# A gated linear attention and its feed-forward layer on one core: units of three chunks in a hand-written order, against single chunks in an order planned by the program

## The chip, the core and the metric

The kernel runs on one core of a Trainium2 chip (trn2). The metric is the device time of one execution in microseconds (us); smaller is better. The program is one instruction stream for each engine: TensorE (PE in the profile, its weight loads PEld), VectorE (DVE), ScalarE (ACT), GpSimd (POOL) and SyncE (SP). Each engine works through its stream strictly in the order in which the kernel wrote it, so an instruction that waits holds up all that stands behind it on that engine. SP only issues transfers (DMAs); POOL issues some too, beside its own arithmetic.

## What is computed

Inputs are q, k, v, a_re and a_im, each of shape (4, 8, 768, 48): 4 batches, 8 heads, 768 steps, 48 channels; and a feed-forward layer with weights of 384x1536 and 1536x384. For each batch and head a 48x48 state is decayed by a complex gate, gets the product k v added, and is read with q. Cut to what matters:

```python
mag = np.sqrt(a_re * a_re + a_im * a_im)
scale = np.minimum(mag, 0.999) / (mag + 1e-06)
a_re_n, a_im_n = (a_re * scale, a_im * scale)
for t in range(S):
    new_re = ar * S_re - ai * S_im
    new_im = ar * S_im + ai * S_re
    S_re, S_im = (new_re + kv, new_im)
    y[:, :, t] = np.einsum('bhd,bhde->bhe', q[:, :, t], S_re)
...
xn = (x - mu) / np.sqrt(var + 1e-06) * g_ln
out = x + np.maximum(xn @ w_ch1, 0.0) @ w_ch2      # x: the 8 heads of y side by side, (4, 768, 384)
```

Both kernels turn the recurrence into a product over chunks of 128 steps. With L the running sum of ln(magnitude) and theta the running sum of the angles, q is multiplied by exp(L)cos(theta) and exp(L)sin(theta), k by exp(-L) and the same two, and a masked 128x128 product of the two takes the place of the loop inside a chunk. A state of 128x384 (decayed by the last row of exp(L), called the edge) goes from one chunk to the next. There are 24 chunks, 6 in each batch.

## The kernel before

A *unit* is three chunks; there are eight. The gate work of a unit is done on 128x1152 tiles (three chunks wide):

- `e_ln` (L175): ACT takes Ln of a_re and Exp of minus that, which is 1/a_re. `e_r` (L180): DVE forms r = a_im/a_re and r squared. `e_l1p` (L185): ACT takes Ln(1 + r squared). `e_lm` (L188): DVE adds 2 Ln(a_re) and caps the sum. So the magnitude comes from a_re and the ratio.
- `e_exp` (L198): per chunk, a matmul with a triangular matrix makes the running sum, ACT takes Exp with both signs; after the unit's last chunk a small DMA on SP (L207) fetches the edge row.
- `e_atan`, `e_carry`, `e_phase`, `e_trig` (L210 to L249): arctan, running sum of angles in turns (carried from chunk to chunk through `carry`), ACT moves it out of PSUM with 768 added (tile w), three DVE operations on the low 16 bits fold it to one turn (f, g), ACT takes two Sin.
- `e_qk`, `e_stack` (L251 to L262): DVE multiplies q and k with exp, sine and cosine: six products in bf16.
- `heads_t` (L264): 16 transposes on PE into two PSUM tiles; ACT copies one out (qt, L273), DVE the other (kt).

Then per chunk: `scores` (L278: 8 matmuls, DVE applies the mask), `values` (L289: y, the state's update, and at a unit's first chunk the decay from the edge, L308 to L312), `norm_t` (L329: x is transposed on PE, DVE copies it out as xt and takes mean and variance). Per unit and block of 128 hidden columns: `up` (L346: three matmuls of 384 columns, ACT applies Relu). Per chunk `down` (L358: 12 matmuls, DVE adds the residual, SP stores).

ACT needs one set of tables for Ln and Exp and another for arctan and sine; `table` (L164) loads them.

The order is written by hand: `put(s, i, f, ...)` (L401) hangs gate work on slot i of step s, and the loop over steps (L467) interleaves it with `values`, `up`, `norm_t`, `scores` and `down`. `up` runs a unit behind, `down` two units behind. For batch b the gates of both its units start five steps before (LEAD, L24). `fold` (L134), which works the layer-norm gain and mean into w1c, is put at step 3 (L423), but its first multiplications depend only on the weights' arrival and may be written earlier into DVE's stream.

Transfers: a_re and a_im go through SP, one DMA of 1,024 rows of 192 bytes for each chunk; q, k, v go through POOL, which converts them to bf16 on the way, also one for each chunk. Two buffers hold units of a_re and a_im, three those of q, k, v. `gln` and `w1c` (L128, L129) come behind the 18 loads of units 0 and 1 on POOL; `w2b` (L132) at step 0.

Of the kernel before, what the change touches and what calls it, by code (L numbers as in the profile page):

```python
# [11 lines left out]
F16 = mybir.dt.float16  # L12
# [3 lines left out]
PI = 3.14159265358979323846  # L16
LNCAP = -0.0020010006671670786
TWO_PI_SAFE = 6.2831845
PI_SAFE = 3.14159225

TURNS = 768.0
TURN = 1 << 14
INV2PI = 1.0 / (2.0 * PI)
LEAD = 5  # L24
MM, SM = 3, 3
NOSYNC = mybir.DependencyInfo(mybir.DependencyClass.NoSync, mybir.DependencyReason.DATA)
# [3 lines left out]
def kernel(  # L30
# [15 lines left out]
    NCH = S // C  # L46
    DM = H * D
# [4 lines left out]
    UC = 3  # L52
    NU = NCH // UC
    UT = UC * C

# [6 lines left out]
    xs = pool("xs", 10)  # L62
    moe = pool("moe", 2)


    units = [{"b": U // NU, "u": U % NU, "U": U} for U in range(B * NU)]
    source = {"ar": (a_re, FP32, nc.sync, 2), "ai": (a_im, FP32, nc.sync, 2),
              "q": (q, BF16, nc.gpsimd, 3), "k": (k, BF16, nc.gpsimd, 3),
              "v": (v, BF16, nc.gpsimd, 3)}

    def load(U, names, c=None):
        if U >= B * NU:
            return
        st = units[U]
        for n in names:
            ap, dt, eng, bufs = source[n]
            view = ap[st["b"]].rearrange("h (c p) d -> p h c d", p=C)
            if n not in st:
                st[n] = ins.tile([C, H, UC, D], dt, tag=n, name=n, bufs=bufs)
            for i in range(UC) if c is None else (c,):  # L80
                eng.dma_start(out=st[n][:, :, i], in_=view[:, :, st["u"] * UC + i])  # L81


    for c in range(UC):
        load(0, ("ar", "ai"), c)
    ident = consts.tile([C, C], BF16)
    make_identity(nc, ident)
    u_half = consts.tile([C, C], BF16)
    make_upper_triangular(nc, u_half, val=0.5, diag=True)
    u_turn = consts.tile([C, C], BF16)  # L90
    make_upper_triangular(nc, u_turn, val=INV2PI, diag=True)
    mask = consts.tile([C, C], BF16)
    make_upper_triangular(nc, mask, val=1.0, diag=True)

    def const(val, shape, dt=FP32, name=None):
        t = consts.tile(shape, dt, name=name)
        nc.vector.memset(t, val)
        return t

    one_b = const(1.0, [C, 1], name="one_b")  # L100
    turns = const(TURNS, [C, 1], name="turns")
    pi_b = const(PI_SAFE, [C, 1], name="pi_b")
    mhalf_pi = const(-PI / 2.0, [C, 1], name="mhalf_pi")
    all_turn = const(INV2PI, [C, C], BF16, name="all_turn")
    ones = const(1.0, [C, C], BF16, name="ones")
    mhalf = const(-0.5, [C, UC], name="mhalf")

    kstks, edgs = [], []
    qstk = consts.tile([C, UC, H, 2, DP], BF16)
    nc.vector.memset(qstk[:, :, :, :, D:DP], 0.0)  # L110
    for i in range(2):
        ks = consts.tile([C, UC, H, 2, DP], BF16, name=f"kstk{i}")
        nc.vector.memset(ks[:, :, :, :, D:DP], 0.0)
        kstks.append(ks)
    for i in range(4):
        ed = consts.tile([UC * H, DP], BF16, name=f"edge{i}")
        nc.vector.memset(ed, 0.0)
        edgs.append(ed)

    load(0, ("q", "k", "v"))  # L120
    load(1, ("ar", "ai"))
    load(1, ("q", "k", "v"))


    w1c = consts.tile([C, ND, DF], BF16)
    w2b = consts.tile([C, NJ, DM], BF16)
    gln = consts.tile([C, ND], FP32)
    nc.gpsimd.dma_start(out=gln, in_=moe_g_ln.rearrange("(i p) -> p i", p=C))  # L128
    nc.gpsimd.dma_start(out=w1c, in_=moe_w_ch1.rearrange("(i p) j -> p i j", p=C))  # L129

    def load_w2():
        nc.gpsimd.dma_start(out=w2b, in_=moe_w_ch2.rearrange("(j p) e -> p j e", p=C))  # L132

    def fold(n):  # L134
        blk = w1c[:, :, ts(n, 512)]
        for i in range(ND):
            nc.vector.tensor_scalar(out=blk[:, i], in0=blk[:, i], scalar1=gln[:, ds(i, 1)],
                                    scalar2=None, op0=ALU.mult)
        ps = psum.tile([C, 512], FP32, tag="mm", name="w_ps", bufs=MM)
        for i in range(ND):  # L140
            nc.tensor.matmul(ps, lhsT=ones, rhs=blk[:, i], start=(i == 0), stop=(i == ND - 1))
        mean = moe.tile([C, 512], BF16, tag="mean", name="mean")
        nc.scalar.activation(out=mean, in_=ps, func=AF.Copy, scale=-1.0 / DM)
        for i in range(ND):
            nc.vector.tensor_tensor(out=blk[:, i], in0=mean, in1=blk[:, i], op=ALU.add)


    ALL = slice(0, UC)
    chunks, state, carry = {}, [None], [None]
    chd = lambda t, cs: t[:, :, cs].rearrange("p h c d -> p c h d")  # L150
    row = lambda x, c: x[:, c].rearrange("p h d -> p (h d)")
    fm = lambda x: x.rearrange("p c h d -> p (c h) d")
    small_ps = lambda name, dt=FP32: psum.tile([C, DM], dt, tag="s", name=name, bufs=SM)

    def utile(st, name, dt=BF16, tag=None, bufs=None):
        if name not in st:
            st[name] = el.tile([C, UC, H, D], dt, tag=tag or name, name=name, bufs=bufs)
        return st[name]


    tables = {"exp": "natural_log_exp_and_others", "trig": "trig_and_small"}
    group = [None, []]

    def table(name):  # L164
        p = nc.scalar.preload_act_table_set(tables[name])  # L165
        for i in group[1]:
            tc.add_manual_dep(p.ins, i.name, NOSYNC, reason="table order")
        group[:] = [p, []]

    def act(**kw):  # L170
        i = nc.scalar.activation(**kw)  # L171
        tc.add_manual_dep(i.ins, group[0].ins.name, NOSYNC, reason="table order")
        group[1].append(i.ins)

    def e_ln(st, cs=ALL):  # L175
        ar = chd(st["ar"], cs)
        act(out=ar, in_=ar, func=AF.Ln)
        act(out=utile(st, "rec", FP32, "wide", 3)[:, cs], in_=ar, func=AF.Exp, scale=-1.0)

    def e_r(st, cs=ALL):  # L180
        r, r2 = utile(st, "r")[:, cs], utile(st, "r2", tag="tmp", bufs=4)[:, cs]
        nc.vector.tensor_tensor(out=r, in0=chd(st["ai"], cs), in1=st["rec"][:, cs], op=ALU.mult)  # L182
        nc.vector.tensor_tensor(out=r2, in0=r, in1=r, op=ALU.mult)

    def e_l1p(st, cs=ALL):  # L185
        act(out=chd(st["ai"], cs), in_=st["r2"][:, cs], func=AF.Ln, bias=one_b)

    def e_lm(st, cs=ALL):  # L188
        if "lm" not in st:
            st["lm"] = el.tile([C, H, UC, D], BF16, tag="lm", name="lm")  # L190
        hcd = lambda t: t[:, :, cs].rearrange("p h c d -> p h (c d)")
# [21 lines left out]
    def e_carry(st, cs=ALL):  # L213
        for c in range(cs.start, cs.stop):
            if st["u"] == 0 and c == 0:
                carry[0] = None
# [298 lines left out]
```

## Time and profile before

| what | us |
|---|---|
| two timed runs, median | 259.5 and 260.24, 259.87 |
| span of the profiled execution, first to last instruction | 259.0 |
| busy in that span: PE / DVE / ACT / POOL | 181.4 / 182.3 / 180.5 / 79.5 |
| first matmul of `up` (h_ps, L354) starts | 86.3 |
| last matmul ends | 255.5 |
| w1c lands | 45.7 |

The profiled execution has no timed figure beside its span; the span is 0.9 us under the median of the timed runs. A time in the profile counts from the span's start. "Releaser" is what ended an engine's wait. In the strip of 40 slices each slice is 6.5 us wide and a digit is the busy share in tenths.

### The profile page before, as it was taken

What the parts mean: (1) busy time and instruction counts of PE and PEld (TensorE: products, weight loads), DVE (VectorE), ACT (ScalarE), POOL (GpSimd) and SP (SyncE); (2) the same over time, 40 slices, a digit from 0 to 9 for tenths busy, and PEclk for the clock granted to TensorE, in tenths of its full rate; (3) what the DMA queues carried; (4) which work ended last, traced back from release to release, by engine and by line L of the source; (5) the groups of instructions that cost most, each with busy time, mean ns of one, the idle gap of its engine ahead of it and who ended that gap; (6) DMA issues with size and microseconds to landing.
All of it is one profiled execution on the core that took longest, in us unless ns stands there. A gap on an engine that the chain in (4) does not pass through costs nothing.

```text
span 259.0 us, 4791 instructions
## 1 busy us (share of the span) xinstructions
PE 181.4 (70%) x1844; PEld 123.9 (48%) x1845; DVE 182.3 (70%) x374; ACT 180.5 (70%) x292; POOL 79.5 (31%) x103
## 2 busy tenths in 40 slices
PE   0116600330227976879999599999969999999994
PEld 0004500210226544666666467666647776766662
DVE  4448960930699889999978999986798966663121
ACT  4568820293978989999879999767988645435430
POOL 9944444761453088520450801032000100101000
PEclk9999965555558979999999999999979999999999
DMA  8999999999997699890699950037000101000112
GB/s 119 146 135 135 136 154 184 145 182 156 138 109 153 123 146 90 41 48 30 98 179 203 145 54 32 33 42 67 31 3 0 63 9 55 33 33 34 59 61 91
DMA packets 130551, 23.93 MB, mean 92 GB/s; under 512 B 125536, under 2 KB 130144, under 8 KB 130528
## 3 DMA queue, kind: packets, MB, share of 16 engines
q0 software_dynamic: 76864, 9.44, 57.0%
q1 hardware_dynamic: 53664, 14.18, 30.4%
q8 instruction: 14, 0.23, 0.3%
q14 instruction: 9, 0.07, 0.1%
HBM read 28.31 MB, written 4.72 MB: 128 GB/s over the span
## 4 chain that ended last, share of the span: by engine, by line
PE 39%; ACT 23%; DMA 21%; DVE 11%; issue 3%; POOL 2%; SPq 0%; ACTq 0%; DVEq 0%; POOLq 0%
PE o_ps L364 16%; PE h_ps L354 11%; DMA w1c<-in_moe_w_ch_dram 6%; DMA q<-in_q_dram 6%; DMA ar<-in_a_re_dram 5%; ACT qt L273 4%; ACT ht L356 4%; PE qk_ps L272 4%; DMA k<-in_k_dram 3%; ACT ar L171 2%; DVE qstk L261 2%; ACT L165 2%; ACT rec L171 2%; ACT w L171 2%; PE a_ps L285 2%
## 5 line engine op out<-in xcount | busy, mean ns | idle before, releaser
L354 PE MATMUL h_ps<-xt,w1c 128*128 128x384 bf16 x288 | 57.5, 329 | 1.2 <-ACT qt L273 0.9
L356 ACT ACTIVATE ht<-h_ps 128x384 bf16<-128x384 f32 x96 | 44.6, 505 | 10.0 <-PE h_ps L354 9.9
L364 PE MATMUL o_ps<-w2b,ht 128*128 128x384 bf16 x288 | 50.2, 326 | 0.3 <-ACT ht L356 0.3
L287 DVE TENSOR_TENSOR at<-a_ps,mask 128x512 bf16<-128x512 f32 x48 | 31.6, 678 | 7.3 <-PE a_ps L285 7.3
L364 PEld LDWEIGHTS <-ht 128*128 128x128 bf16 x288 | 27.6, 98 | 17.2 <-issue 0.4
L81 POOL DMA_DIRECT2D v<-in_v_dram x24 | 21.3, 895 | 46.3 <-PE t_ps L318 27.9
L354 PEld LDWEIGHTS <-w1c 128*128 128x128 bf16 x288 | 26.6, 98 | 17.3 <-issue 3.8
L81 POOL DMA_DIRECT2D k<-in_k_dram x24 | 21.8, 921 | 29.3 <-DVE en L255 13.2
L201 PE MATMUL l_ps<-lm,u_half 128*128 128x384 bf16 x24 | 7.9, 365 | 32.5 <-DVE lm L195 30.3
L367 DVE SCALAR_TENSOR_TENSOR o<-o_ps,rs,x 128x384 f32<-128x384 f32 x24 | 14.7, 614 | 21.6 <-PE o_ps L364 19.3
L273 ACT COPY qt<-qk_ps 128x1024 bf16<-128x1024 bf16 x24 | 24.3, 1024 | 6.0 <-PE y_ps L299 3.3
L341 POOL TENSOR_SCALAR rs<-mv 128x3 f32<-128x3 f32 x8 | 3.3, 410 | 76.2 <-DVE dec L311 54.9
L272 PE MATMUL qk_ps<-ident,qstk 128*128 128x128 bf16 x192 | 17.1, 240 | 12.4 <-DVE qstk L261 11.6
L171 ACT ACTIVATE ep<-l_ps 128x384 bf16<-128x384 f32 x24 | 12.2, 508 | 16.4 <-PE l_ps L201 16.3
L81 POOL DMA_DIRECT2D q<-in_q_dram x24 | 21.9, 924 | 5.5 <-DMA k<-in_k_dram 4.5
L302 ACT CAST x<-y_ps 128x384 bf16<-128x384 f32 x24 | 11.7, 489 | 16.3 <-PE y_ps L299 14.2
L182 DVE TENSOR_TENSOR r<-ai,rec 128x1152 bf16<-128x1152 f32 (+1 forms) x10 | 11.1, 1109 | 14.8 <-ACT rec L171 8.1
L272 PEld LDWEIGHTS <-qstk 128*128 128x128 bf16 x192 | 14.0, 109 | 15.2 <-DVE qstk L261 13.2
L230 PE MATMUL th_ps<-r,u_turn 128*128 128x384 bf16 x24 | 8.9, 394 | 15.6 <-ACT r L171 8.4
L285 PE MATMUL a_ps<-qt,kt 128*128 128x128 bf16 x192 | 17.5, 223 | 2.3 <-DVE at L287 1.7
L334 PEld LDWEIGHTS <-x 128*128 128x128 bf16 x72 | 5.8, 101 | 27.6 <-issue 23.8
L273 DVE COPY kt<-qk_ps 128x1024 bf16<-128x1024 bf16 x24 | 16.2, 680 | 2.9 <-PE qk_ps L272 2.9
(79 smaller groups left out, 390.2 us busy)
## 6 DMA issues: line engine op xcount, KB each, us to landing
ar<-in_a_re_dram SPq DMA_DIRECT2D x24, 192.0 KB, 4.5
ai<-in_a_im_dram SPq DMA_DIRECT2D x24, 192.0 KB, 8.2
out_dram<-o SPq DMA_DIRECT2D x24, 192.0 KB, 1.9
q<-in_q_dram POOLq DMA_DIRECT2D x24, 96.0 KB, 4.9
k<-in_k_dram POOLq DMA_DIRECT2D x24, 96.0 KB, 9.5
v<-in_v_dram POOLq DMA_DIRECT2D x24, 96.0 KB, 5.9
w1c<-in_moe_w_ch_dram POOLq DMA_DIRECT2D x1, 1152.0 KB, 16.3
w2b<-in_moe_w_ch_dram POOLq DMA_DIRECT2D x1, 1152.0 KB, 15.1
```

The source lines that it names most:

```text
L81: eng.dma_start(out=st[n][:, :, i], in_=view[:, :, st["u"] * UC + i])
L171: i = nc.scalar.activation(**kw)
L182: nc.vector.tensor_tensor(out=r, in0=chd(st["ai"], cs), in1=st["rec"][:, cs], op=ALU.mult)
L272: nc.tensor.transpose(t_ps[:, h], x[:, c, h].rearrange("p a d -> p (a d)"), ident)
L273: copy(out=o, in_=t_ps)
L285: nc.tensor.matmul(a_ps[:, j], lhsT=ch["kt"][:, h], rhs=ch["qt"][:, h], start=True, stop=True)
L287: nc.vector.tensor_tensor(out=at[:, ts(i, H // 2)], in0=a_ps, in1=mask_b, op=ALU.mult)
L302: nc.scalar.copy(out=x, in_=y_ps)
L354: nc.tensor.matmul(h_ps, lhsT=w1c[:, i, ts(j, C)], rhs=st["xt"][:, i], start=(i == 0), stop=(i == ND - 1))
L356: nc.scalar.activation(out=st["ht"][:, j], in_=h_ps, func=AF.Relu)
L364: nc.tensor.matmul(o_ps, lhsT=st["ht"][:, j, ts(c, C)], rhs=w2b[:, j], start=(j == 0), stop=(j == NJ - 1))
L367: nc.vector.scalar_tensor_tensor(out=o, in0=o_ps, scalar=st["rs"][:, ds(c, 1)], in1=chunks[U * UC + c]["x"], op0=ALU.mult, op1=ALU.add)
```

## The change

The kernel is rewritten; the algorithm of the chunks stays. What differs:

1. **A planner.** Each piece of work is declared with engine, an assumed duration, what it needs and makes, and a due time; `Plan.order` runs a list schedule on these assumed times and the instructions are written in that order. The transfers of a queue are modelled as a ring of their own (`QY`, `QP`); issuing one is assumed to cost 0.1 us on SP and 0.9 us on POOL.
2. **Chunks, not units.** `up` works on one chunk: 36 matmuls of 128 columns each instead of 36 of 384 for three chunks; ACT applies Relu to 1,024 and 512 columns at once. Gates are worked in groups: chunks 0; 1 and 2; 3 to 5 of batch 0, then three at a time.
3. **Magnitude from the sum of squares.** m2 = a_re² + a_im², L = half of Ln(m2); 1/a_re = Exp(-0.5 Ln(a_re²)). In batch 0 ACT squares and DVE adds and multiplies; from batch 1 on GpSimd does all four operations (two squares, the sum, the angle's ratio), and the adding of carries.
4. **Phases from mid-batch.** From batch 1 on the running angle starts at the batch's middle and runs backwards over its first half (`u_back`, `all_back`), so that 192 turns added to it keep enough bits; DVE moves it out of PSUM with that addition, ACT takes Sin of the low 16 bits directly, and DVE adds a quarter turn for the second. Only group 2 (`far`) still shifts.
5. **Smaller moves.** The first step of `fold` goes from DVE to ACT. From chunk 10 on x is transposed by a DMA issued on SP, not on PE. The loads of w1c and w2b move ahead on POOL, and one DMA loads all six chunks of a tensor for batches 2 and 3.

The core of the diff:

```diff
+    def load(eng, b, names, c=None, after=()):
+            op(eng, 0.1 if eng is Y else 0.9 if c is not None else 4.0, list(before.get(eng, ())) + list(after),
+               [key] + [("in_" + n, b)], load_fn, eng, b, n, c)
+            plan.add(RING[eng], (2.04 if b < 2 else 1.5) * len(cs), None, [key],
+                     [("got_" + n, b, i) for i in cs], lag=2.0)
...
-    def e_ln(st, cs=ALL):
-        ar = chd(st["ar"], cs)
-        act(out=ar, in_=ar, func=AF.Ln)
-        act(out=utile(st, "rec", FP32, "wide", 3)[:, cs], in_=ar, func=AF.Exp, scale=-1.0)
...
+    def gate_exp(G, eng, early):
+        n, g = G["n"], G["i"]
+        sb = 0.2 + 0.32 * n
+        slow = 0.1 + 0.42 * n if eng is V else 0.2 + 0.8 * n
...
+        sq = (A, sb) if eng is V else (eng, slow)
+        op(*sq, got("ar"), [("ar2", g)], e_ar2, uses=[in_("ar")])
+        op(*sq, got("ai"), [("ai2", g)], e_ai2, uses=[in_("ai")])
+        op(eng, slow, [("ar2", g), ("ai2", g)], [("m2", g)], e_m2, uses=[in_("ar")])
+        act(sb, [("ar2", g)], [("ln", g), rw], e_ln, uses=[in_("ar")])
+        act(sb, [("ln", g)], [("rec", g)], e_rec, uses=[rw])
+        op(eng, slow, got("ai") + [("rec", g)], [("r", g)], e_r, uses=[in_("ai"), rw])
+        act(sb, [("m2", g)], [("lm0", g)], e_lm, **kw)
+        op(V, 0.1 + 0.13 * n, [("lm0", g)], [("lm", g)], e_cap, **kw)
...
+        op(Y, 0.1, [("ep", g), ("consts",)], [("edge", g)], e_edge, lag=2.5)
...
+            op(V, 0.1 + 0.42 * m, [("th_ps", g, j)], [("w", g), rw], e_turn, j, m, **kw)
...
+        act(sb, [src], [("sin", g)], e_sin, "sin", uses=[rw], **kw)
+        op(V, 0.1 + 0.21 * n, [("w", g), ("sin", g)], [("w2", g)], e_quarter, uses=[rw], **kw)
...
+        if j == 0:
+            op(T, 0.1, [("edge", G["i"])], [("e_ps", g)], decay, takes="nar")
+            op(V, 0.12, [("e_ps", g)], [("dec", G["i"])], decay_out)
...
+        if g < PE_X:
+            op(T, 0.18, [("x", g)], [("x_ps", g)], x_turn, takes="nar")
+            op(V, 0.36, [("x_ps", g)], [("xt", g)], xt_out)
+        else:
+            op(Y, 0.1, [("x", g)], [("xt", g)], xt_dma, lag=3.0)
...
+        for j0, j1 in ((0, 8), (8, 12)):
+            op(T, 0.163 * (j1 - j0), [("xt", g)] + w1, [("h_ps", g, j0)], up, j0, j1,
+               takes="wide" if j1 - j0 > 4 else "nar")
+            op(A, 0.2 + 0.107 * (j1 - j0), [("h_ps", g, j0)], [("ht", g)], relu, j0, j1)
...
+        op(T, 1.97, [("ht", g), ("W2",)], [("o_ps", g)], down, takes="nar")
+        op(V, 0.61, [("o_ps", g), ("rs", u), ("x", g)], [("o", g)], residual)
+        op(Y, 0.1, [("o", g)], [("out", g)], store, due=40.0 + STEP * g)
...
+    for c in range(GMAX):
+        load(Y, 0, ("ar", "ai"), c)
+    op(P, 1.5, [], [("consts",)], constants)
+    load(P, 0, ("q", "k", "v"), 0)
+    load_w(P, 0.1, ("gln",), gln, moe_g_ln.rearrange("(i p) -> p i", p=C))
+    load(P, 0, ("q", "k", "v"), 1)
+    load_w(P, 10.0, ("W1",), w1c, moe_w_ch1.rearrange("(i p) j -> p i j", p=C))
+    load(P, 0, ("q", "k", "v"), 2)
+    for c in range(GMAX, NCH):
+        load(Y, 0, ("ar", "ai"), c)
+    load(P, 0, ("q", "k", "v"), 3)
+    load_w(P, 12.0, ("W2",), w2b, moe_w_ch2.rearrange("(j p) e -> p j e", p=C))
+    for c in range(GMAX + 1, NCH):
+        load(P, 0, ("q", "k", "v"), c)
+    for c in range(NCH):
+        load(Y, 1, ("ar", "ai"), c, [("edge", 0)] if c < 3 else [("edge", 1)])
+        load(P, 1, ("q", "k", "v"), c)
+    for b in range(2, B):
+        load(Y, b, ("ar", "ai"))
+        load(P, b, ("q", "k", "v"))
...
+    phases = [([G], V) for G in groups[:3]] + [([G], P) for G in groups[3:5]] + [
+        (groups[2 * b + 1:2 * b + 3], P) for b in range(2, B)]
...
+    done = plan.order(SLOTS)
+    with tc.manual_schedule():
+        for o in done:
+            if o["fn"]:
+                o["fn"][0](*o["fn"][1])
```

Here V, A, P, T and Y are DVE, ACT, POOL, PE and SP; `STEP` is 6.9, `PE_X` 10. Groups are numbered 0 to 8; group 3 is the first of batch 1. Buffers of each of the five inputs hold a whole batch, two of them.

## The prediction

> **What bounds the kernel now.** First the strip of 40 slices on the profile's page. Read it for where PE, which does most of the arithmetic, is idle.
>
> ```profile
> PE   0116600330227976879999599999969999999994
> DVE  4448960930699889999978999986798966663121
> ACT  4568820293978989999879999767988645435430
> POOL 9944444761453088520450801032000100101000
> PEclk9999965555558979999999999999979999999999
> DMA  8999999999997699890699950037000101000112
> ```
>
> PE is nearly idle for thirteen slices (some 85 us) and nearly full afterwards; in that first part the transfers are full and PE's clock drops to half. The table of stretches puts numbers on both parts (columns: length, then busy us and count for PE, PEld, DVE, ACT, POOL; clock, DMA share, GB/s). The cut is the start of the first `up` matmul.
>
> ```profile
> 0.00:86.30 86.30, 26.51 (x263) 18.71 (x265) 50.74 (x118) 52.68 (x75) 43.70 (x59) 0.74 1.57 142
> 160.00:259.00 99.00, 91.57 (x900) 61.93 (x897) 63.07 (x124) 58.29 (x106) 7.19 (x11) 0.98 0.16 40
> ```
>
> Before 86.3 us PE is busy 26.5 us; from 160 on it is busy 91.6 of 99.0, a share of 0.925. So the kernel is a slow start of 86 us and then a stream in which PE sets the pace (ACT was close to full from 86 to 160). What a chunk costs PE is read late in its timeline, where no gate work runs: the first matmul of `values` in two successive steps.
>
> ```profile
> 222.54 0.19 PE L296 MATMUL y_ps<-v,at 128*128 128x48 bf16 x1
> ...
> 228.05 0.19 PE L296 MATMUL y_ps<-v,at 128*128 128x48 bf16 x1
> ```
>
> The step takes 5.5 us. To it come the transposes of `heads_t` (16 in 0.89 us at full clock) and three matmuls for the gates (0.5 us together): 6.9 us a chunk, of which `up` and `down` are 3.9. Times 24, less about 3 us for first and last chunks of a batch: 163 us for PE.
>
> Why the start is slow shows in the timelines of DVE and ACT, where a bracket holds the idle time before an instruction and what ended it:
>
> ```profile
> 45.72 1.18 DVE L137 TENSOR_SCALAR w1c<-w1c,gln 128x512 bf16<-128x512 bf16 x3 [9.38 <-DMA w1c<-in_moe_w_ch_dram]
> ...
> 63.10 1.16 ACT L171 ACTIVATE ar<-ar 128x1152 f32<-128x1152 f32 x1 [4.14 <-DMA ar<-in_a_re_dram]
> ```
>
> DVE stood before `fold`'s first step until w1c landed; the cap of unit 1 (L193) stood behind it, its buffers came free late, the next a_re was issued at 48 us and ACT waited for it until 63. POOL's and SP's own timelines say why transfers are late:
>
> ```profile
> 29.36 0.77 POOL L129 DMA_DIRECT2D w1c<-in_moe_w_ch_dram  x1 [1.06 <-DMA q<-in_q_dram]
> ...
> 45.90 0.91 POOL L81 DMA_DIRECT2D v<-in_v_dram  x1 [3.65 <-DMA w1c<-in_moe_w_ch_dram]
> ...
> 64.00 0.87 POOL L81 DMA_DIRECT2D k<-in_k_dram  x1 [6.84 <-DMA w2b<-in_moe_w_ch_dram]
> ```
>
> ```profile
> 13.12 7.16 SPq L81 DMA_DIRECT2D ai<-in_a_im_dram  x3
> 20.40 2.08 SPq L207 DMA_DIRECT2D edge<-ep  x1
> 22.58 4.94 SPq L81 DMA_DIRECT2D ar<-in_a_re_dram  x3
> 27.57 9.83 SPq L81 DMA_DIRECT2D ai<-in_a_im_dram  x3
> ...
> 52.00 11.10 SPq L81 DMA_DIRECT2D ai<-in_a_im_dram  x3
> 63.20 2.24 SPq L207 DMA_DIRECT2D edge<-ep  x1
> ```
>
> Count POOL's issues: w1c is the 20th, and the 28th waits for it; w2b is the 30th, and the 38th waits for it. Every wait there fits "number n is issued once number n-8 has landed". So POOL, as an engine, is held at the speed of the transfers, about 1.85 us for each load of q, k or v (16 landings from 11.9 to 39.6). SP's issues are held too: 12 loads take until 20.3, the next six from 22.6 to 37.4, and an edge waits its turn (ready at 53, issued at 63.2).
>
> **The change, part by part.**
>
> *Earlier weights.* w1c becomes POOL's 8th issue instead of its 20th. By the landings above (third load 11.9, six by 17.5) and its own 6 us (39.6 to 45.7) it lands at about 24, not 45.7. `fold`, now 9 ACT instructions of some 0.6 us (the mean's row, 128x512, 0.645) and 9 DVE ones of 0.417, ends near 34. Moved past on POOL: 12 loads, which land later (chunk 2's by 30, chunks 3 to 5 behind w2b's 7.7 us by 54), still before the 69 us below. Nothing else of the old chain (DVE behind w1c, buffers, ACT behind a_re) returns, because two buffers now hold whole batches. What is late next is the edge.
>
> *Edges on SP.* Edge 0 stands behind the same 12 loads: 20.4, as before, landing 22.5. Edge 1 stands behind six more (22.6 to 37.4): 39.5. Edge 2 behind the next six, at the same 14.9 us: 56. The planner assumes 0.1 us an issue, so DVE's copy `dec` and PE's `decay` are written early into in-order streams: quarter turn, masks and copies queue behind dec. On its clock dec of group 2 comes near 37; that is 19 us of slip.
>
> *Gate products on POOL.* The planner assumes 36 loads at 0.9 and three at 0.8: issued by 36 us, products of group 3 from about 40. By the rule read above, the 39th waits for the 31st, that is 28 loads and all weights; before, 27 loads and all weights had landed at 64.0. So POOL's first product starts near 66.5, its end near 69. ACT's Ln of group 3 waits for it, written (by the assumed times) near 43, after one to two chunks of `up` and `down`. Behind it on ACT stand Relu, qt and x of the following chunks, and PE waits for those. This takes in the edges' slip.
>
> The product itself has no row. Below: DVE's r on the same 128x1152 floats, 1.34 us. Above: POOL's select on 128 elements, 0.28 us, scaled to 1152 (2.55) and doubled for the second input, 5.1. I take 2.6, as a one-input POOL row is nearest. 24 products and some 11 carry additions (0.9) are 72 us, room enough from 66 on; at 5.1 they are about 140, the last group is through near 209, and 34 us of chain and chunks follow: 243.
> The Trainium skill, GPSIMD Engine Reference, section "Elementwise — side-by-side cycle accounting", gives 4497 ns for 2,048 floats, which would be an estimate of 2.5 us here; no run shows it yet.
>
> *DVE and POOL at once.* The cap of 128x384 took 0.73 us while POOL issued a DMA (10.55 to 11.49), 0.26 without:
>
> ```profile
> 10.85 0.73 DVE L195 TENSOR_SCALAR lm<-lm 128x384 bf16<-128x384 bf16 x1
> ...
> 15.39 0.26 DVE L195 TENSOR_SCALAR lm<-lm 128x384 bf16<-128x384 bf16 x1
> ```
>
> So DVE can lose up to half a POOL instruction; beside the issue at 22.25 a product of `e_qk` (0.34 at 22.62) lost nothing. Two operations a group (cap, quarter turn) lose 1.3 at most: 12 x 1.3 = 16 us, which DVE's slack takes. Zero is the other end.
> The Trainium skill, SBUF — State Buffer, section "Practical consequences", says that a DVE instruction with two SBUF inputs contends with a GpSimd one that reads SBUF, the second to issue being blocked until the first is done. By it the six products of `e_qk` and `e_stack` are exposed too and the sum would lie between this forecast and the last rival's; the row above, beside a descriptor write, neither bears it out nor excludes it.
>
> *Engine totals.* DVE loses r, r squared and the sum (1.34 + 0.75 + 1.34 a unit) and the folding (0.88 + 0.51 + 0.45), gets the move out of PSUM (about 1.5 a unit; its nearest row is s, 0.547 for 384) and the quarter turn (0.45 to 0.88): -3 a unit, -24; batch 0's sums and ratios +5; fold -4; 14 copies of xt -5: from 182 to about 155, of which some 45 fall before 69 us. ACT: w goes (-13.1), Relu of 1,024 and 512 columns costs 1.02 + 0.63 (qt's and the mean's rows) against 1.86 (-5), paired Exp -3, squares +5, fold +5, one table load +1.3: from 180 to 171. PE: `up` in 128 columns costs 36 x 0.056 = 2.0 a chunk (qk_ps: 16 in 0.89) against 1.94 (+1); transposes gone -2: 163 stays.
>
> *Transposes by DMA.* No row. Below: a store lands in 1.9 us; above: a loaded ai took 15.1. I take 3, near an unloaded a_re load (2.7), since batch 3's loads should be out by chunk 10. Between `values` and `up` of a chunk lies about one period of 7 us, so 3 costs nothing; each us over 7 costs 14.
>
> **The sum.** At 69 us PE has done attention for about four chunks (4 x 2.9) and 1.5 chunks of `up` and `down` (6): 17.5 of 163. The other 145.5 at the old share of 0.925 take 157. The tail after the last matmul stays 3.5 (255.5 to 259.0). Span 69 + 157 + 3.5 = 229.8; the profiled span lies 0.9 under the median of 259.87, so the median becomes 231. With a share between 0.90 and 1.0, and the hold at 69 some us either way, 216 to 242.
>
> **Rivals.**
> - *No hold.* If issues on POOL don't hold the products (they come ahead of the last loads, or ACT's Ln stands later), only edge 1 delays: the stream starts near 40 with 10 us of PE done: 40 + 153/0.925 + 4.4 = 210; 203 to 216. For: the data of group 3 is there by 40. Against: POOL's waits.
> - *POOL slow, or SP held.* Products at 5.1 give 243. Batch 2's loads on SP, six chunks in one issue, can stand before stores: 12 x 1.2 to 2.5 us (14.9 for six, above), and once three output buffers are full residuals wait, up to 15 more. 242 to 254.
> - *Little change.* The slips of edges (19) and POOL (26) add up instead of overlapping, with the Ln written ahead of any `up` at 43: start at 43 + 45 = 88 with 10 us of PE done, 88 + 165 + 4.4 = 258.
> - *Slower: transposes by DMA.* If they land in over 9.4 us, 14 x 2.4 = 34 is added and the time passes 265. For: loaded landings of 8 to 15. Against: the DMA strip is nearly empty after slice 26.
> - *Slower: DVE and POOL shut each other out.* All 72 us of POOL then add to DVE's 110 after 69: 182/0.925 = 197, ending at 270; with 67 it passes 265. If only eight operations a group meet POOL, busy 72 of 157 us, and wait half a product: 48 x 0.46 x 1.3 = 29, and 139 still lies under PE's 145.
>
> **How the numbers follow.** Chances: forecast 0.45, no hold 0.22, POOL or SP 0.13, little change 0.08, slower 0.12 (0.07 the transposes, 0.05 the exclusion). Within 2% of 259.87 is 254.7 to 265.1, about what a measurement of this kernel can tell from no change. Faster: 0.45 + 0.22 + 0.13 = 0.80. A range of 206 to 258 leaves out a quarter of "no hold", half of "little change" and "slower": 2 in 10.
>
> **What would show it.** w1c's landing near 24 and the first `up` before 50; POOL idle before its issues until about 66 and its first square there; ACT idle before Ln of group 3, released by POOL, until 69; edges issued near 20, 37 and 54; from 70 on PE busy above 0.9 at full clock, 6.5 to 7 us a chunk. Wrong would be: products on POOL before 50 (then 210), DVE or PE held regularly by POOL or by a transpose's landing (then 245 and more).

## The result, and the profile after

The changed kernel takes 278.78 us (median of 277.77 and 279.79) against 259.87 before: a ratio of 1.0716, 95% interval 1.0606 to 1.0826. It is slower, and outside the forecast's range of 206 to 258. The profiled execution spans 278.0 us. Some executions of a kernel, in the sets below, run over 1.5% longer than its fastest; times and ratios given here are of the others, a time as their median, but the traces of two of the runs below, b2 (256.7) and e1 (267.4), are of longer ones.

The strip of 40 slices on the page of the changed kernel, each slice now 6.95 us:

```profile
PE   0000040479388378679895945999998859899984
DVE  1500061578949959945897299779827696961821
ACT  4410079379926586487659973779987547545240
POOL 8935313536994678729583993420620320010010
PEclk9999999999779779959999595899999799999999
DMA  9999999999981942998699000192111010111121
```

PE is nearly idle for eight slices (some 55 us), and its first `up` starts at 67.4, near the forecast 69. What was not forecast is the middle: from the eleventh slice to the twenty-fifth PE's digit goes up and down between 3 and 9 and its clock drops again, while POOL, which had little to do there before, is busy. The table of stretches, cut at 70 us in both kernels (columns: length, then busy us and count for PE, PEld, DVE, ACT, POOL; clock, DMA share, GB/s), first after, then before:

```profile
0.00:70.00 70.00, 19.67 (x182) 13.66 (x182) 25.88 (x60) 35.21 (x47) 36.20 (x51) 1.00 1.65 149
70.00:180.00 110.00, 80.51 (x975) 62.54 (x971) 84.35 (x118) 75.77 (x93) 75.11 (x39) 0.83 0.81 91
70.00:280.00 210.00, 166.34 (x2204) 133.52 (x2199) 146.78 (x222) 135.42 (x168) 90.77 (x53) 0.90 0.55 71
```

```profile
0.00:70.00 70.00, 17.80 (x163) 11.68 (x163) 36.03 (x93) 38.75 (x57) 37.17 (x52) 0.75 1.63 148
70.00:280.00 210.00, 163.64 (x1681) 112.26 (x1682) 146.28 (x282) 141.77 (x236) 42.31 (x51) 0.96 0.54 65
```

At 70 us both kernels have about the same PE work behind them (19.7 and 17.8 us) and the same before them (166.3 and 163.6). The old kernel needs 189 us for the rest (to 259.0), a PE share of 0.866; the new one 208 (to 278.0), a share of 0.80. So the start, which the change was to shorten, is neither better nor worse at 70, and the 19 us that were lost lie behind it: PE idles 42 us there, not 25.

What happened in the start shows in the timelines. POOL (a bracket holds the idle time before and what ended it):

```profile
20.86 0.88 POOL L205 DMA_DIRECT2D q<-in_q_dram  x1 [4.21 <-DMA w1c<-in_moe_w_ch_dram]
...
40.66 0.87 POOL L205 DMA_DIRECT2D k<-in_k_dram  x1 [7.11 <-DMA w2b<-in_moe_w_ch_dram]
...
69.22 1.05 POOL L205 DMA_DIRECT2D v<-in_v_dram  x1 [1.26 <-DMA q<-in_q_dram]
70.28 2.12 POOL L345 TENSOR_TENSOR ar<-ar 128x1152 f32<-128x1152 f32 x1
```

w1c was there at 20.9, and POOL's first product starts at 70.28, right behind its last held issue: the rule "n waits for n-8" gave 66.5. But ACT didn't wait for these products. The first Ln of group 3, which needs the square that ends at 72.4, stands in ACT's timeline without a wait before it:

```profile
91.50 1.16 ACT L358 ACTIVATE rec<-ar 128x1152 f32<-128x1152 f32 x1
```

The edges, on SP, PE, DVE and ACT:

```profile
25.53 1.87 SPq L386 DMA_DIRECT2D edge<-ep  x1
```

```profile
35.51 0.21 PE L561 MATMUL e_ps<-ident,edge 8*64 8x8 bf16 x2 [21.25 <-DMA edge<-ep]
50.75 0.22 PE L561 MATMUL e_ps<-ident,edge 16*64 16x16 bf16 x2 [9.32 <-DMA edge<-ep]
```

```profile
36.23 0.52 ACT L460 ACTIVATE cos<-w 128x384 bf16<-128x384 int16 x1 [20.83 <-DVE w L464]
...
46.99 1.93 ACT L267 ACTIVATE w1c<-w1c,gln 128x512 bf16<-128x512 bf16 x3
```

Edge 0 is issued at 25.5 and lands at 35.4, 9.9 us later; until then PE, DVE and ACT stand for some 20 us, and `fold`, whose weights lie ready, runs at 47 to 64 instead of ending near 34. The first `up` (67.4) follows from that. The chain of work that ended last, followed back from the last instruction, says the same. Its five longest pieces (start, us, what):

```profile
13.17 7.67 SPq L205
25.53 9.93 DMA edge<-ep
43.89 6.81 DMA edge<-ep
70.47 5.22 DVE r L364
90.85 5.00 DVE qstk L494 x2
```

SP's loads and the two edges make its start; POOL's loads don't stand in it. Its last two are DVE operations that took several times their own length beside POOL; more on them below.

### The profile page after: what moved, and what is told of

It is laid out like the page before. It is cut to its first block, busy times and chain, and to the rows that moved or that the text cites. A ratio compares the mean times of both kernels' runs of the same rounds, so it can differ in the third digit from the quotient of the medians.

```text
span 278.0 us, 5649 instructions
## 1 busy us (share of the span) xinstructions
PE 186.0 (67%) x2378; PEld 147.2 (53%) x2378; DVE 172.7 (62%) x281; ACT 170.6 (61%) x214; POOL 127.0 (46%) x103
## 4 chain that ended last, share of the span: by engine, by line
PE 37%; DVE 22%; ACT 15%; DMA 10%; SPq 9%; issue 5%; POOL 1%; DVEq 0%; ACTq 0%
PE h_ps L642 13%; PE o_ps L657 12%; SPq L205 9%; DMA edge<-ep 7%; PE qk_ps L517 5%; DVE at L534 4%; DVE qstk L494 3%; DVE w L451 3%; ACT qt L521 2%; DMA xt<-x 2%; ACT ht L646 2%; DVE r L364 2%; PE a_ps L530 2%; DVE o L661 2%; DVE en L489 2%
## 5 line engine op out<-in xcount | busy, mean ns | idle before, releaser
L642 PE MATMUL h_ps<-xt,w1c 128*128 128x128 bf16 x864 | 56.4, 226 | 10.5 <-DVE xt L619 5.8
L642 PEld LDWEIGHTS <-w1c 128*128 128x128 bf16 x864 | 52.7, 101 | 12.5 <-DVE xt L619 5.2
L657 PE MATMUL o_ps<-w2b,ht 128*128 128x384 bf16 x288 | 54.7, 344 | 2.8 <-ACT ht L646 1.5
L646 ACT ACTIVATE ht<-h_ps 128x512 bf16<-128x512 f32 (+1 forms) x48 | 38.0, 811 | 25.9 <-PE h_ps L642 25.7
L534 DVE TENSOR_TENSOR at<-a_ps,mask 128x1024 bf16<-128x1024 f32 x24 | 28.7, 1218 | 4.5 <-PE a_ps L530 4.5
L364 POOL TENSOR_TENSOR r<-ai,rec 128x1152 bf16<-128x1152 f32 x6 | 16.2, 2699 | 17.8 <-ACT rec L361 17.8
L460 ACT ACTIVATE cos<-w 128x1152 bf16<-128x1152 int16 (+2 forms) x8 | 8.3, 1040 | 24.7 <-DVE w L464 24.7
L345 POOL TENSOR_TENSOR m<-ai 128x1152 f32<-128x1152 f32 x6 | 13.1, 2182 | 12.6 <-ACT lm L368 12.6
L604 DVE BATCH_NORM_STATS2 s<-x 128x6 f32<-128x384 bf16 x24 | 13.1, 546 | 8.1 <-ACT x L550 8.1
L530 PE MATMUL a_ps<-qt,kt 128*128 128x128 bf16 x192 | 15.6, 230 | 3.5 <-ACT qt L521 2.4
```

The costliest lines, as they stand in the source:

```text
L345: eng.tensor_tensor(out=out, in0=in_, in1=in_, op=ALU.mult)
L364: eng.tensor_tensor(out=hm(theta(G)), in0=merged(part(G, "ai")), in1=hm(f32(G, "rec")), op=ALU.mult)
L530: T.matmul(ch["a"][:, h], lhsT=ch["kt"][:, h], rhs=ch["qt"][:, h], start=True, stop=True)
L534: V.tensor_tensor(out=ch["at"], in0=ch["a"], in1=K["mask"].unsqueeze(1).to_broadcast([C, H, C]), op=ALU.mult)
L642: T.matmul(ps[:, jj], lhsT=w1c[:, i, ts(j0 + jj, C)], rhs=ch["xt"][:, i], start=(i == 0), stop=(i == ND - 1))
L646: A.activation(out=ch["ht"][:, j0:j1], in_=ch["h", j0][:, 0:j1 - j0], func=AF.Relu)
```

## The experiments

The kernels were run beside the kernel before, whose median was 260.7 to 261.9 us in these sets; ratios are to it, with 95% intervals. "Residual n" is the start of DVE's residual of chunk n, the end of a chunk's work. The planner's clock is the sum of its own assumed times: it is no measurement, but says where the written order would end if they held. For the changed kernel it ends at 241.6, with residual 0 at 52.3.

### Two holds in parallel?

The first theory: the edges' transfers and POOL's products are two holds side by side, so that only both edits together help. The rivals: one alone carries it, or the planner's wrong issue times (0.1 us on SP, 0.9 on POOL) spoil the order.

```diff
a1_edge, a3_both
-            Y.dma_start(out=G["edge"][0:n * H, 0:D],
+            A.dma_start(out=G["edge"][0:n * H, 0:D],
a2_dve, a3_both: squares, sum and ratio of batches 1 to 3, in the same written order
-                eng.tensor_tensor(out=out, in0=in_, in1=in_, op=ALU.mult)
+                V.tensor_tensor(out=out, in0=in_, in1=in_, op=ALU.mult)
a4_true
-            op(eng, 0.1 if eng is Y else 0.9 if c is not None else 4.0,
+            op(eng, 2.1 if eng is Y and b < 2 else 1.0 if eng is Y else 1.85 if c is not None else 2.4,
...
-        op(Y, 0.1, [("ep", g), ("consts",)], [("edge", g)], e_edge, lag=2.5)
+        op(Y, 0.1, [("ep", g), ("consts",)], [("edge", g)], e_edge, lag=7.0 if g < 2 else 2.5)
```

> The changed kernel, same written order, but the edge rows are fetched by DMAs issued on ACT instead of SP. Theory 'late start in two places': the edges (35.4 us for the first, planned 12.5) and POOL's loads (first gate product at 70.3, planned 37.1) hold the streams one after the other, in parallel rather than in sum; with the edges gone DVE's 20.9 us wait at 14.9 goes, but group 3's products still start near 66 to 70 and everything behind them stays some 30 us late: 266 to 279. Rival 'the edges alone': the 22.9 us that the first edge is late come off the end: 254 to 258.

> The changed kernel, same written order, but the four gate products of batches 1 to 3 are computed on DVE (24 operations of about 1.36 us) instead of POOL. Theory 'late start in two places': POOL's hold goes, the edges' hold of about 27 us stays: 266 to 276. Rival 'DVE and POOL shut each other out': DVE's stretched rows (r 5.22, en mean 1.42, qstk mean 1.27, fr mean 1.67 us) fall back to 1.35, 0.75, 0.75 and 0.88, some 17 us, and with POOL's wait gone too the time falls below 260. Rival 'DVE becomes the bound': 33 us of work more on DVE, over 279.

> Both edits: edges issued on ACT, gate products on DVE, same written order. Theory 'late start in two places': the slip against the planner's own clock (34 us at the end) falls to about 10, and the time comes near the planner's own end of 241.6: 245 to 258. If the stream itself were slower than planned (exclusion aside), it stays above 262.

> The changed kernel with only the planner's assumed times of issuing corrected to what the profile shows (SP 2.1 us and POOL 1.85 us for each load of batches 0 and 1, first two edges 7 us), so that the order is written for late edges and products. The planner's own end is then 255.9 instead of 241.6. Theory 'the order was planned on wrong times': the run follows the new plan, 255 to 266. Rival 'the transfers are late whatever the order': 272 to 285.

Measured: edges on ACT 278.6 (1.0653, 1.0602 to 1.0703); products on DVE 275.66 (1.0539, 1.0477 to 1.06); both 279.12 (1.0676, 1.062 to 1.0732); corrected issue times 282.8 (1.0814, 1.0761 to 1.0866). Each edit alone came out in the theory's range, but both together bring no more than none (245 to 258 was expected), so the theory fell as it was stated, and with it that correct issue times alone would mend the order. One reason shows in ACT's timeline, in the run with the edges on ACT:

```profile
11.04 0.49 ACT L382 ACTIVATE ep<-l_ps 128x384 bf16<-128x384 f32 x1 [1.01 <-PE l_ps L377]
...
21.91 1.21 ACTq L386 DMA_DIRECT2D edge<-ep  x1
...
47.05 0.57 ACTq L386 DMA_DIRECT2D edge<-ep  x1
```

Edge 0 is ready at 11.5 and issued at 21.9 (on SP: 25.5), the second at 47.1 (43.9). PE has edge 0 at 27.3 instead of 35.5 and edge 1 at 52.5 instead of 50.8: moving the issue to an engine with no loads helped the first and not the second. The Trainium skill, DMA: Bandwidth & Descriptors, section "Issuing engines are not separate DMA queues", says that transfers of all engines run on the same 16 DMA engines and that issuing on several saves only the time of issuing; the trace agrees that little is saved, but here the issue itself waited 10.4 us. That it waited for SP's loads, which were outstanding then, is inferred: the profile names nothing that ended the wait. So neither run had removed the hold.

### Edges without a transfer

To remove it in earnest, the last row of exp(L) is turned into a column by PE itself: one matmul of one column per head, written onto the edge's place. Nothing is left out.

```diff
-                T.matmul(ps[i * DP:(i + 1) * DP, 0:m], lhsT=G["edge"][0:m], rhs=K["ident"][0:m, 0:m],
-                         start=True, stop=True)
+                for e in range(m):
+                    T.matmul(ps[i * DP:i * DP + D, e:e + 1], lhsT=G["row"][:, ts(e, D)],
+                             rhs=K["ident"][:, C - 1:C], start=True, stop=True)
```

> The changed kernel with the edge taken from exp(L) by 16 to 48 one-column matmuls a group instead of by a DMA (some 1.3 us of PE a group), in nearly the same written order; the transfers stay. Theory 'two holds in parallel' (edges, and POOL's loads before group 3's products): the first edge is there at about 12 instead of 35.4, the first store comes some 15 us earlier, but group 3's first product stays near 70 (planned 37.1) and with it the later chunks: 266 to 280. Rival 'edges alone': 22 us come off, near 256.

> Edges by matmul and the gate products of batches 1 to 3 on DVE, nearly the same written order. Theory 'two holds in parallel': both are gone, so the slip against the planner's own end of 241.6 falls from 36 to below 12: 245 to 255. If the time stays above 265, neither hold is the cause and something else at the start (arrival of data of chunks 3 to 5) or the stream decides.

> Edges by matmul, and the planner's assumed issue times corrected (SP 2.1, POOL 1.85 us a load), so that products are planned when POOL is free; the planner's own end is 252.6. Theory 'order planned on wrong times': the time follows within 10 us, 252 to 263. Rival 'late whatever the order': over 270.

Measured: 284.69 (1.0868, 1.0816 to 1.0919); with the products on DVE 277.1 (1.0588, 1.0517 to 1.0659); with corrected issue times 278.84 (1.0646, 1.0599 to 1.0693). The edges are gone from the start (DVE has the first at 14.9, the second at 25.1), PE has done 31.7 us at 70 instead of 19.7, and the time is no better; all three lie above what the theory expected of them. Where it went stands in DVE's and POOL's timelines of the first of these:

```profile
83.58 0.62 DVE L661 SCALAR_TENSOR_TENSOR o<-o_ps,rs,x 128x384 f32<-128x384 f32 x1 [26.75 <-POOL rs L610]
```

```profile
74.47 0.89 POOL L205 DMA_DIRECT2D v<-in_v_dram  x1
75.36 2.14 POOL L345 TENSOR_TENSOR ar<-ar 128x1152 f32<-128x1152 f32 x1
77.43 2.13 POOL L345 TENSOR_TENSOR m<-ai 128x1152 f32<-128x1152 f32 x1
79.64 2.61 POOL L354 TENSOR_TENSOR m<-m,ar 128x1152 f32<-128x1152 f32 x1
82.33 0.24 POOL L609 TENSOR_SCALAR rs<-mv 128x3 f32<-128x3 f32 x1
82.65 0.89 POOL L610 TENSOR_TENSOR rs<-rs,mhalf 128x3 f32<-128x3 f32 x1
```

DVE stood 26.75 us before its first residual. It waited for `rs`, the norm's scale of chunks 0 to 2: an operation of 1.1 us on POOL which stands behind all of POOL's loads and three products. While DVE stood, ACT waited 25.1 us for DVE's `fr` and PE 24.5 us for DVE's `w`. With the products on DVE the scale was still on POOL, behind the loads: DVE waited 11.0 us for it, and the first residual came at 75.9. So once the edges are gone, POOL's held issues hold the core by the scale, which none of the edits so far had touched. In the changed kernel itself DVE waited 0.3 us for it: there the edges' hold hides it.

### POOL's issues taken away

Four runs follow from that. Three leave out the 24 loads of q, k and v of batches 1 to 3 (batch 0's are read again), which takes 24 of POOL's 45 issues away and keeps the written order; two leave out the scale (DVE copies the variance instead).

```diff
d1_noqkv, d2_noqkv_mm, d3_free
+        if b and n in ("q", "k", "v"):
+            inp[n, b] = inp[n, 0]
+            return
d3_free, e1_rs
-            P.tensor_scalar(out=t, in0=stats[u][:, :, 1], scalar1=1e-6, scalar2=None, op0=ALU.add)
-            P.tensor_tensor(out=t, in0=t, in1=K["mhalf"], op=ALU.pow)
+            V.tensor_copy(out=t, in_=stats[u][:, :, 1])
```

> Leaves out the 24 loads of q, k and v for batches 1 to 3 (batch 0's are read again); every other instruction and the written order stay. In the run with edges by matmul, DVE stood 26.8 us before its first residual because the norm's scale is computed on POOL, behind POOL's loads, and POOL's products stand there too. Theory 'issues': POOL's held issues put a constant slip on the whole list. With 21 issues instead of 45, POOL's first product starts near 45 us instead of 70, the first residual comes at 55 to 65 instead of 82, and the time falls to 248 to 258. Theory 'order': PE's share of 0.80 after the start comes from the written order itself and an earlier start is eaten by waits later on: first residual early as well, time still 268 to 280.

> As the run without loads of q, k and v for batches 1 to 3, and the edges come by one-column matmuls instead of transfers on SP. Theory 'issues': both holds are gone, the slip against the planner's own clock (which ends at 241.6) should be under 10: 242 to 252, and 4 to 8 us under the run that keeps the transferred edges. Theory 'order': within 4 us of that run, and over 265.

> As the run without loads of q, k and v for batches 1 to 3 and with edges by matmul; the gate products also run on DVE, and the norm's scale is left out (DVE copies the variance in its place), so that POOL has next to no work. Theory 'issues': what POOL does beside DVE costs little once it isn't late; within 5 us of the run with edges by matmul, 242 to 252. A third theory, 'sharing' (DVE held beside POOL's products, some 17 us of DVE in the changed kernel, sets the pace of the stream): 8 us or more under that run. Theory 'order': over 262.

> All loads are kept. Edges by matmul, gate products on DVE, and the norm's scale left out (DVE copies the variance in its place), so that POOL does nothing but issue loads and no engine waits for POOL's arithmetic. Theory 'issues': the 11 us for which DVE waited for the scale in the same kernel with the scale on POOL (278.1) come out in full: first residual near 65, time 264 to 269. Theory 'order': the first residual moves, the end does not: 274 to 280.

| run | us | ratio, interval | residual 0 | last residual |
|---|---|---|---|---|
| changed kernel | 278.78 | 1.0716, 1.0606 to 1.0826 | 82.4 | 274.3 |
| without loads (d1) | 267.91 | 1.0295, 1.0223 to 1.0367 | 81.9 | 265.7 |
| the same, edges by matmul (d2) | 256.1 | 0.9801, 0.975 to 0.9853 | 63.5 | 251.7 |
| the same, products on DVE, no scale (d3) | 264.54 | 1.0134, 1.0093 to 1.0175 | 66.1 | 257.5 |
| all loads, edges by matmul, products on DVE, no scale (e1) | 263.82 | 1.011, 1.0073 to 1.0148 | 66.3 | 261.9 |

The residuals are of the profiled executions. The last run came out at the lower end of what held issues gave (264 to 269): its ratio is 0.048 under that of the same kernel with the scale on POOL (1.0588), some 12 us, near the 11 us of wait that were taken away. The first missed what held issues gave (248 to 258): its products start at 48.0 instead of 70.3 (they now wait for a_re, on SP), but the edges still hold the start, its first residual stays at 81.9, and it gained 11 us. The gain doesn't come from the start: its residuals are level with the changed kernel's up to chunk 1 and 8.4 us ahead at chunk 6. The second gained another 12 and is 4.1 over its 252. So the two holds do lie in parallel: taking away the edges' transfers alone gained nothing (284.7), POOL's loads alone 11 us, both 23. The caution: leaving loads out also takes their traffic away; the run with all loads and no scale is free of that.

The third run was to test the rival that DVE held beside POOL sets the pace. It is 8 us slower than the second, so moving the products to DVE costs more than it gives. But it adds some 33 us of work to DVE, so it doesn't show that the holding is free; its time also lies where the order's theory put it (over 262). The traces say more. In the changed kernel, DVE and POOL:

```profile
70.47 5.22 DVE L364 TENSOR_TENSOR r<-ai,rec 128x1152 bf16<-128x1152 f32 x1
```

```profile
70.28 2.12 POOL L345 TENSOR_TENSOR ar<-ar 128x1152 f32<-128x1152 f32 x1
72.35 2.12 POOL L345 TENSOR_TENSOR m<-ai 128x1152 f32<-128x1152 f32 x1
74.54 3.62 POOL L354 TENSOR_TENSOR m<-m,ar 128x1152 f32<-128x1152 f32 x1
```

The ratio took 5.22 us where 1.34 is its time alone: it begins 0.2 us behind POOL's first square and ends 1.2 us behind the second. The sum that POOL then begins takes 3.62 instead of 2.61. Over the whole run such stretched DVE instructions add up to some 18 us, and PE stood behind the two longest, this one and a product of 0.75 us that took 4.42:

```profile
77.34 2.74 PE L642 MATMUL h_ps<-xt,w1c 128*128 128x128 bf16 x24 [5.07 <-DVE xt L619]
95.91 1.89 PE L517 MATMUL qk_ps<-ident,qstk 128*128 128x128 bf16 x16 [4.62 <-DVE qstk L494]
```

Some 12 of the 18 us lie on the chain that ended last. So the rival isn't refuted: sharing with POOL cost the changed kernel time, how much no run separates.

### Is it the order?

Even with both holds gone (d2) the stream runs at 8.2 us a chunk (63.5 to 251.7 in 23 steps), and that is the pace of the planner's own clock (52.3 to 240.7). On that clock PE works 160.7 of the 200 us from the first `up` (41.6) to the end (241.6), a share of 0.80. To tell the order from the work, one number of the planner was changed in d2's kernel, so that the same instructions come out in an order that its clock ends 22.6 us later.

```diff
-            gate_trig(G, eng, 5.0 if G["b"] else 0.0)
+            gate_trig(G, eng, 10.0 if G["b"] else 0.0)
```

> The run without loads of q, k and v for batches 1 to 3 and with edges by matmul (256.7 us; the planner's own clock ends at 241.6), with one number changed: the head start that the planner gives the stacking of later batches' gates is 10 instead of 5 us. The same instructions come out in another order, which ends at 264.2 on the planner's clock, 22.6 later. Theory 'list' (time is the planner's own end plus a slip that arises at the start, 15 us here): 274 to 284. Theory 'work' (the engines' work, the granted clock and DVE beside POOL set the pace, and the order matters little): 254 to 264.

Measured: 271.4 (272.36 and 270.46), some 15 over the same work in the other order. That is 3 under the range that the order's theory gave and 7 over that of the work. PE's busy time was the same in both, 194.2 and 195.0 us. So the written order alone is worth some 15 us here. Its residuals start 11.7 us behind their plan and end 3.5 behind it, which is why 22.6 on the planner's clock became 15. What no run shows is a better order: whether these pieces, chunk by chunk, can be written as tightly as the old units stays open.

What this doesn't settle: the slip against the planner's clock stays near constant in the changed kernel (30 at residual 0, 36 at chunk 4, 34 at the last) and without loads and edges (11 and 11). With corrected issue times it is 4 us at residual 0 and 22 at the last (57.6 against 61.4, 255.0 against 276.9), and with the edges by matmul as well (c3) 5 and 22, so the edges don't bring these 16 to 18 us. In that last run the slip is 23 by chunk 8, and by then DVE operations beside POOL had taken some 18 us more than their own length. Three in a row, 0.75 each alone:

```profile
100.20 2.65 DVE L492 TENSOR_TENSOR qstk<-qe,sin 128x1152 bf16<-128x1152 bf16 x1
102.78 2.65 DVE L492 TENSOR_TENSOR kstk<-en,sin 128x1152 bf16<-128x1152 bf16 x1
105.36 2.65 DVE L492 TENSOR_TENSOR qstk<-qe,cos 128x1152 bf16<-128x1152 bf16 x1
```

PE waited 4.8 us for them. The planner's assumed times know nothing of DVE and POOL sharing; that this is the whole of the slip is not shown.

### The change's parts in the order by hand

```diff
b1_edge, b4_edge_w1
-            nc.sync.dma_start(out=st["edge"][:, 0:D],
+            nc.scalar.dma_start(out=st["edge"][:, 0:D],
b2_w1, b4_edge_w1: behind load(0, ("q", "k", "v")) instead of behind unit 1's
+    nc.gpsimd.dma_start(out=gln, in_=moe_g_ln.rearrange("(i p) -> p i", p=C))
+    nc.gpsimd.dma_start(out=w1c, in_=moe_w_ch1.rearrange("(i p) j -> p i j", p=C))
b3_pool
-        nc.vector.tensor_tensor(out=r, in0=chd(st["ai"], cs), in1=st["rec"][:, cs], op=ALU.mult)
-        nc.vector.tensor_tensor(out=r2, in0=r, in1=r, op=ALU.mult)
+        eng = nc.gpsimd if st["U"] > 3 else nc.vector
+        eng.tensor_tensor(out=r, in0=chd(st["ai"], cs), in1=st["rec"][:, cs], op=ALU.mult)
+        eng.tensor_tensor(out=r2, in0=r, in1=r, op=ALU.mult)
```

> The kernel before with two edits: w1c loaded behind unit 0's nine loads on POOL instead of behind eighteen, and edges issued on ACT. Theory: DVE's wait of 9.4 us for w1c, and behind it unit 1's cap, unit 3's a_re and ACT until 63, go; PE's start moves up by about 10: 248 to 254. Rival 'unit 1's q, k, v now come later and take its place': 257 to 266.

> The kernel before, in its order by hand, with one part: edges issued on ACT's queue instead of SP's. Together with the weights behind unit 0 it gave a ratio of 0.968. If the edges, issued 8 to 10 us late behind SP's loads before, carried that gain: 252 to 256. If DVE behind w1c carried it: 258 to 262.

> The kernel before, in its order by hand, with the other part: w1c loaded on POOL behind unit 0's nine loads instead of 18. If DVE's 9.4 us of waiting for w1c carried the gain: 251 to 256. If the edges on SP carried it: 257 to 262.

> The kernel before, in its order by hand, with the ratio and its square of units 4 to 7 on POOL: 4 x (1.34 + 0.75) = 8.4 us less of DVE, 4 x (2.6 + 2.1) = 19 us more of POOL, and ACT's next step of a unit comes about 2.6 us later. If work on POOL is worth as much here as in the list (8 us between the run with the products on DVE and the run with them on POOL): 255 to 259. If the later step for ACT or DVE held beside POOL costs more than it gives: 262 to 270.

Measured: both (b4) 253.21 (0.9682, 0.9642 to 0.9723), edges alone (b1) 261.99 (1.0044, 1.0016 to 1.0073), early w1c alone (b2) 251.4 (0.9631, 0.9542 to 0.972), products on POOL (b3) 270.27 (1.0373, 1.0294 to 1.0453). The early weights carry the whole gain, and the version with them is faster than both kernels. DVE no longer waits for w1c: its multiplication follows the scores' mask at once,

```profile
38.10 0.68 DVE L287 TENSOR_TENSOR at<-a_ps,mask 128x512 bf16<-128x512 f32 x1
38.70 0.87 DVE L137 TENSOR_SCALAR w1c<-w1c,gln 128x512 bf16<-128x512 bf16 x3
39.50 1.36 DVE L193 SCALAR_TENSOR_TENSOR lm<-ar,ai 128x1152 bf16<-128x1152 f32 x1
```

the first `up` starts at 81.6 instead of 86.3, and the last residual comes 4.0 us earlier. The edges on ACT give nothing here either.

Products on POOL cost 9.5 us in this order. ACT and DVE of that run:

```profile
126.18 1.26 ACT L171 ACTIVATE ai<-r,one_b 128x1152 f32<-128x1152 bf16 x1 [3.17 <-POOL r L184]
```

```profile
121.56 2.62 DVE L194 SCALAR_TENSOR_TENSOR lm<-ar,ai 128x1152 bf16<-128x1152 f32 x1
```

A unit's ratio and square take 2.63 + 2.1 or more on POOL, not 2.09 on DVE, two units in a row come 5.3 us later, ACT waits for them with Relu behind it, and a DVE instruction beside them took 2.62 instead of 1.34. Against the kernel before, the residuals come 4.1 us later after the first such pair (chunk 1) and 12.5 after the second (chunk 8), where it stays (this execution took 273.1).

## Why the prediction was wrong, by its own steps

- **Weights:** right. w1c was there at 20.9 (forecast 24). **`fold` by 34 and `up` before 50:** wrong. `fold` stands on ACT behind work that the first edge held, and ran at 47 to 64; `up` began at 67.4. In the order by hand the same step was worth 0.9631.
- **Edges on SP:** the issue times were near (25.5 and 43.9; 20 and 37 forecast), the landing was not: 9.9 us instead of 2.1 for edge 0, and it held ACT beside DVE and PE. The slip of 19 us was put on edge 2, read as planned near 37; on the planner's clock its copy stands at 65.0. The slip came from edge 0, planned for 12.5 and there at 35.4: 23 us. The size was right by luck.
- **POOL's hold:** right in rule and size (66.5 forecast, 70.3), wrong in what it holds. The text has ACT's Ln of group 3 written near 43; on the planner's clock it stands at 61.3, and in the trace at 91.5, 19 us after its square was done, without a wait. What held PE until 67.4 was the edges and `fold` behind them. So the start near 69 came true by luck. What POOL's queue can hold is the norm's scale, which was not named: it shows once the edges are gone.
- **The product's price:** 2.6 taken; 2.6 for sum and ratio, 2.1 for a square. The Trainium skill, GPSIMD Engine Reference, section "Elementwise — side-by-side cycle accounting", gives 4497 ns for 2,048 floats, an estimate of 2.5 here, and the trace agrees.
- **DVE and POOL at once:** the 16 us were the right size (some 18), the operations wrong: products with two inputs are held too, r for 3.9 us. That is what the Trainium skill says in SBUF — State Buffer, section "Practical consequences", and the rows at 70.47 us agree with it. That DVE's slack takes it was wrong too: some 12 us of it lie on the chain that ended last. The 72 us of the last rival were far too much.
- **DVE's total:** 172.7, not 155, for these 18 us. ACT's: 170.6, as forecast (171).
- **DMA transposes:** landings of 2.3 to 3.6 us, 3 taken; PE waited 1.8 us for them in all. That rival fell.
- **The step that failed:** "The other 145.5 at the old share of 0.925 take 157". It took 208 (70 to 278, the tail with it). Both factors were mis-sized. PE's work from 70 us on was 166.3 us, not 145.5: the forecast summed rows at full clock, and the granted clock was 0.90 there (166.3 x 0.90 = 150; in the old kernel 0.96 and 163.6). At the forecast share that is 22 us more. The share was 0.80, not 0.925, and that is another 28. The old kernel's own share was not far off: cut at 70 it is 0.866 (163.6 of 189), which still holds 16 us of its slow start, and from its first `up` at 86.3 on it is 0.90 (154.9 of 172.7). So the larger part goes with the new order: its plan, computed by the kernel's own planner, has PE at 0.80 before any wait that the planner doesn't know. How much of the measured 0.80 is the order and how much the sharing of DVE and POOL is not separated.
- **The likeliest case's premise**, that PE runs as closely after the hold as the old stream did, gave the new order the old one's tightness without a reason. The forecast did price the slip at the start, but not that the rest of the order is no tighter than its plan: on the planner's own clock the stream needs 8.2 us a chunk, and the chip did 8.3 (82.4 to 274.3). That clock ends at 241.6 with neither hold in it, 12 above the 229.8 that was forecast with a hold until 69.

## What to carry to other kernels

Where a program plans the order, read its own clock first: it gave the end and PE's share without any wait that it doesn't know. Cut the profile before at the time at which the changed stage ends, and take PE's remaining work from that cut, not from rows at full clock. When an engine's queue is held by its DMA issues, list everything else on that queue, the small operations too: in the run with edges by matmul, 1.1 us of GpSimd work in the wrong place stopped DVE for 26.8. When a large rewrite bundles a good part with a new order, run the part alone: the early weights alone were worth 4%, and the rewrite with them in it lost 7%.

## What the runs showed of the hardware

- The issue of a DMA on ACT waited while SP's loads were outstanding: ready at 11.5, issued at 21.9. In the order by hand the first edge was issued there at 16.6, as soon as its row was ready.
- A transfer of 0.8 KB landed 9.9 us after its issue behind loads of 192-byte rows.
- GpSimd on 128x1152 f32: 2.1 us for a square (both inputs the same), 2.6 for two inputs; the ratio on DVE 1.34 alone and 5.22 beside two GpSimd squares.
- PE's clock falls back in the middle of a stream that waits: after 5.1 us of idling, 24 matmuls of `up` took 2.74 us at 77.34, at a granted clock of 0.50; at 111.25, at clock 1.00, the same 24 took 1.50. There the order cost twice, by the wait and by the slower matmuls behind it.
